# A scan-and-GeGLU kernel: the first weight rows second in the load queue, an activation tile on another queue, and tile 0's first products ahead of tile 1's transposes

## The chip, the core and the metric

The kernel runs on one NeuronCore of one Trainium2 chip. The metric is the device time of one execution in microseconds (us), the median of several executions; lower is better. Short names for the engines: PE is TensorE (matmul; PEld its weight loads), DVE VectorE, ACT ScalarE, POOL GpSimd, SP SyncE.

## The reference

```python
xn = _layernorm(x)                       # x: 1 x 2048 x 512, eps 1e-5, no affine part
s = _A_ref(xn, ...)                      # diagonal complex state space layer, 512 states
g = _silu((_gelu(xn @ w_gate) * (xn @ w_up)) @ w_down)      # F = 1376
return x + s * g
...
def _A_ref(x, ...):
    dt = exp(log_dt); Lam_bar = exp(dt * Lam); B_bar = ((Lam_bar - 1) / Lam)[:, None] * Bmat
    h_t = Lam_bar * h_{t-1} + B_bar x_t          # over 2048 steps
    y_t = 2 Re(C h_t) + Dskip * x_t
```

All inputs and the output are bfloat16.

## The kernel before

The 2048 tokens are four groups of 512, and each group is four tiles of 128 tokens. Per tile there are the products with w_up and w_gate (four row blocks of 128, columns cut at 512, 1024 and 1376), the GELU and the product of both on ACT and DVE, a transpose by DMA, and the product with w_down. Per group there are the products with B, a rotated real scan on DVE in place of the complex recurrence, and the products with C. PE is the engine that is hardly ever idle.

The program is written as a list of steps; each step belongs to an engine and emits its instructions. `Plan.run` emits them in the order of the tuple `ORDER`, which is written out in full. Each engine executes its own steps strictly in that order, so a step that waits holds up everything behind it on its engine. Nothing in `ORDER` is decided at run time; the times given to `load_x`, `load_w`, `dma` and the like are remarks of the plan and change no instruction.

This document is about the first microseconds, group 0, whose tiles are prepared by hand instead of by DMA:

- SP issues the loads one after the other: `load_x` (line 222) loads one tile of x (128 x 512, 128 KB), `load_w` (line 213) a block of a weight. The first 1024 columns of w_up come as four row blocks of 256 KB, called blocks 0 to 3 here; the other columns, the last tile of x, w_gate and B follow. ACT issues three loads of 1 KB each (line 256: log_dt, Lambda_im, Lambda_re).
- `dummies` (line 299) and `fill` (line 303) are products of constants which PE runs while nothing has landed. Their results are not used.
- `center(m)` takes the mean of tile m (tile 0: lines 339 and 341, shared by ACT and DVE; tiles 1 and 2: line 347 on ACT) and subtracts it on DVE (lines 343 and 348) into `xna`.
- `head_t(m)` transposes the centred tile on PE into PSUM and copies it into `xcT` (shown as the tile W, whose memory it uses): tile 0 in two halves, PE line 313, copies on DVE (line 319) and ACT (line 321); tiles 1 and 2 whole, PE line 328, copy on DVE (line 330).
- `parameters()` transposes the three small loads on PE (lines 603 and 604) and casts them on DVE (line 606); POOL and DVE go on from there to the decay and the angles.
- `up_rows(m, k)` (line 388) multiplies tile m by block k of w_up: two products of 512 columns, accumulated over k in two PSUM banks. `squares(m)` (line 352, ACT) and `stats(m)` (lines 280 and 281, DVE) give the variances; POOL makes the scale (lines 289 to 292), and ACT applies it when it evicts the finished sums (`out_up`, line 398).
- `first_w` (line 418) are the remaining products of group 0 with w_up and w_gate.

PE's order at the head is: `dummies`, `fill`, the transposes of tile 0, the transposes of tile 1, `parameters`, `up_rows(0, 0)`, the transposes of tile 2, `up_rows(1, 0)`, `(1, 1)`, `(0, 1)`, `(2, 0)`, `(2, 1)`, `(0, 2)`, `(1, 2)`, `(0, 3)`, `(1, 3)`, `(2, 2)`, `(2, 3)`, then `first_w`. DVE's is: centring of tile 0, centring of tile 1, copy of tile 0's first half, centring of tile 2, copy of tile 1, parameter cast, copy of tile 2. ACT's is: mean part of tile 0, mean of tile 1, mean of tile 2, copy of tile 0's second half, squares of tiles 1 and 2.

The loads report to eight semaphores in turn; a later load is issued on one of them only when the earlier load on the same one has landed.

Of the kernel before, what the change touches and what calls it, by code (L numbers as in the profile page):

```python
# [17 lines left out]
PE, ACT, DVE, POOL, SP = "PE", "ACT", "DVE", "POOL", "SP"  # L18


ORDER = (
# [23 lines left out]
)  # L45


# [33 lines left out]
def kernel(  # L81
# [17 lines left out]
    nc = tc.nc  # L99
    P = 128  # L100
    S = 2048
    D = 512
    F = 1376
    KT = D // P
# [3 lines left out]
    TS = 512  # L108
# [12 lines left out]
    V, A, G, T = nc.vector, nc.scalar, nc.gpsimd, nc.tensor  # L121
# [9 lines left out]
    x_tok = sb("x_tok", [P, NS * M, D])  # L131
    xnT = sb("xnT", [P, 2, M, KT, P])
    wg = sb("wg", [P, KT, F])
    wu = sb("wu", [P, KT, F])
# [3 lines left out]
    pv0, pv1 = sb("pv0", [4, P]), sb("pv1", [8, P])  # L138
# [52 lines left out]
    def dma(eng, issue, land, emit, reads=(), writes=(), **kw):  # L191
        return pl.add(eng, issue, emit, reads, writes, lag=land, **kw)

    TURN, SLAB = (3, 2.28, 1.5), (2, 1.5, 1.0)
    x_r = A_x[0].rearrange("(m p) d -> p m d", p=P)
# [14 lines left out]
    def load_w(nm, k0, k1, c0, c1, end, landed):  # L210

        w, r = w_of[nm]
        dma_sp(end, landed, lambda: nc.sync.dma_start(out=w[:, k0:k1, c0:c1], in_=r[:, k0:k1, c0:c1]),
               [(nm, k, c) for k in range(k0, k1) for c in range(3) if c0 <= CH[c][0] < c1])
# [6 lines left out]
    def load_x(m, end, landed):  # L221
        dma_sp(end, landed, lambda: nc.sync.dma_start(out=x_tok[:, m, :], in_=x_r[:, m, :]), [("x", 0, m)])  # L222

    W2 = CH[1][1]
    load_x(0, 1.12, 2.92)
    load_x(1, 1.59, 3.35)
    load_x(2, 2.06, 3.75)
    load_w("wu", 0, 1, 0, W2, 2.53, 5.1)
    load_w("wu", 1, 2, 0, W2, 3.0, 6.3)
    load_w("wu", 2, 3, 0, W2, 3.5, 7.4)  # L230
    load_w("wu", 3, 4, 0, W2, 4.0, 7.9)
    load_w("wu", 0, KT, W2, F, 4.5, 9.2)
    load_x(3, 5.0, 9.6)
    load_w("wg", 0, KT, 0, TS, 5.5, 11.0)
    load_w("wg", 0, KT, TS, F, 6.0, 13.5)
    for ri, src in enumerate((A_B_re, A_B_im)):
        dma(SP, 2.0, 3.0, lambda ri=ri, src=src: nc.sync.dma_start_transpose(out=BT[:, ri, :, :], in_=src), writes=[("BT", ri)],
            after=list(sp_last), svc=TURN)
# [13 lines left out]
    one = nc.const_aps.tensor(1.0, [P, 1], FP32)  # L252

    first = [acts(1, lambda: act(out=tiny[:], in_=one, func=AF.Silu), [], ["tiny"], rank=910.0, not_before=0.72)]
    for i, (t, v) in enumerate(((pv0[0:4, :], A_log_dt), (pv1[0:4, :], A_Lambda_im), (pv1[4:8, :], A_Lambda_re))):
        first = [dma(ACT, 0.48, 1.7, lambda t=t, v=v: A.dma_start(out=t, in_=v.rearrange("(k p) -> k p", p=P)),
                     writes=[("pv", i)], rank=900.0, not_before=0.8, after=first)]
    iota_i = sb("iota_i", [P, NBA], I32)
    iota_f = small("iota_f", NBA)

# [41 lines left out]
    def fill(w, i):  # L302
        pe(1, w, lambda: T.matmul(ring[i][:, 0:w], lhsT=warm[:, 0:P], rhs=warm[:, 0:w], start=True, stop=True), [], [("bank", i)])
# [347 lines left out]
    fill(256, 3)  # L651
    center(0)
    head_t(0)
    parameters()
    for m in range(1, M - 1):
        center(m)
# [187 lines left out]
```

## Time and profile before

| | us |
|---|---|
| median of 3 runs (lowest to highest) | 178.61 (178.25 to 178.89) |
| the profiled execution, its own time | 178.7 |
| its span in the trace | 176.9 |
| PE busy | 172.5 |
| DVE busy | 157.0 |
| ACT busy | 123.6 |
| POOL busy | 11.3 |

The span runs from the first to the last instruction of the program in the trace; the execution's own time contains 1.8 us more. All times inside the execution are counted from the start of the span. Matmuls are pipelined, so the duration shown for one contains its latency, and the distance from start to start says more. The mean granted clock of the profiled execution was 0.998.

### The profile page before, as it was taken

To read this page: it belongs to the slowest core of one execution; us is meant where nothing else is said; L and a number is where in the kernel's file an instruction comes from. 1 tells how busy PE (TensorE), PEld (TensorE's weight loads), DVE (VectorE), ACT (ScalarE), POOL (GpSimd) and SP (SyncE) were. 2 spreads that over 40 slices of the span, in tenths; PEclk is the share of its full clock that TensorE was granted. 3 is DMA by queue.
4 is the path that set the end of the run, shared out by engine and by line. 5 is a ranking of instruction groups with operands and counts; after the bars stand their busy time and mean duration, and the time that the engine had idled before them with its cause. 6 is when DMAs were issued, how large, how long until landed. Compare 5 with 4: busy or idle time off the path is not lost.

```text
span 176.9 us, 2419 instructions
## 1 busy us (share of the span) xinstructions
PE 172.5 (98%) x846; PEld 82.5 (47%) x846; DVE 157.0 (89%) x252; ACT 123.6 (70%) x236; POOL 11.3 (6%) x25
## 2 busy tenths in 40 slices
PE   8999999999999999999999999999999999999992
PEld 3454554444455544444445454444444455444451
DVE  2869999999698993999979999899999999999764
ACT  5589979979999999799578855373158618572240
POOL 2580030000200000000040000000000000000000
PEclk9999999999999999999999999999999999999999
DMA  5999999997000809423000075094000006617112
GB/s 145 318 369 241 207 239 261 181 266 163 0 0 0 200 1 186 98 78 63 0 0 6 30 126 105 30 192 85 0 0 0 0 30 156 70 38 157 41 60 77
DMA packets 48355, 18.66 MB, mean 105 GB/s; under 512 B 40312, under 2 KB 47832, under 8 KB 48344
## 3 DMA queue, kind: packets, MB, share of 16 engines
q1 hardware_dynamic: 48320, 18.52, 47.3%
q8 instruction: 6, 0.10, 0.2%
q14 instruction: 5, 0.04, 0.1%
q10 hardware_dynamic: 24, 0.00, 0.0%
HBM read 6.46 MB, written 2.10 MB: 48 GB/s over the span
## 4 chain that ended last, share of the span: by engine, by line
PE 94%; DVE 2%; DMA 1%; ACT 0%; issue 0%; SPq 0%; DVEq 0%
PE ring L449 32%; PE ring L481 22%; PE ring L547 16%; PE ybank L497 15%; PE ring L418 5%; PE ring L388 3%; PE ybank L418 2%; DMA x_tok<-in_A_x_dram 1%; DVE yg L502 1%; DVE junk L508 1%; PE ybank L328 0%; ACT junk L347 0%; SPq L222 0%; DVE xna L348 0%; PE ring L603 0%
## 5 line engine op out<-in xcount | busy, mean ns | idle before, releaser
L449 PEld LDWEIGHTS <-xnT 128*128 128x128 bf16 x288 | 28.2, 98 | 28.4
L481 PE MATMUL ring<-wd,atT 128*128 128x512 bf16 (+1 forms) x176 | 39.3, 379 | 0.0
L449 PE MATMUL ring<-wg,xnT 128*128 128x512 bf16 (+1 forms) x144 | 31.6, 357 | 0.0
L449 PE MATMUL ring<-wu,xnT 128*128 128x512 bf16 (+1 forms) x144 | 31.3, 357 | 0.0
L547 PE MATMUL ring<-xnT,BT 128*128 128x512 bf16 x128 | 30.1, 379 | 0.0
L578 DVE TENSOR_TENSOR_SCAN Fs<-rho,ini,W 128x512 bf16<-128x512 f32 x24 | 29.6, 1269 | 0.1
L452 ACT ACTIVATE ub<-ring 128x512 bf16<-128x512 f32 (+1 forms) x36 | 19.2, 555 | 14.2 <-PE ring L449 14.0
L497 PE MATMUL ybank<-C,hst 128*128 128x512 bf16 x120 | 27.7, 379 | 0.0
L481 PEld LDWEIGHTS <-atT 128*128 128x128 bf16 (+1 forms) x176 | 17.2, 98 | 20.8
L549 ACT ACTIVATE U<-ring 128x512 bf16<-128x512 f32 x32 | 18.3, 600 | 7.5 <-PE ring L547 7.5
L452 ACT ACTIVATE gt<-ring 128x512 bf16<-128x512 f32 (+1 forms) x36 | 19.5, 556 | 3.7 <-PE ring L449 3.5
L497 PEld LDWEIGHTS <-hst 128*128 128x128 bf16 x136 | 13.3, 98 | 14.0
L547 PEld LDWEIGHTS <-BT 128*128 128x128 bf16 x128 | 12.5, 98 | 14.7
L484 ACT ACTIVATE g<-ring 128x512 f32<-128x512 f32 x16 | 9.4, 595 | 14.3 <-PE ring L481 14.2
L559 DVE TENSOR_TENSOR Q<-U,tab 128x4096 bf16<-128x4096 bf16 x8 | 18.3, 2290 | 0.9 <-ACT tab L646 0.7
L559 DVE TENSOR_TENSOR Q<-Fs,tab 128x4096 bf16<-128x4096 bf16 x8 | 18.3, 2286 | 0.1
L502 DVE TENSOR_TENSOR yg<-ybank,g 128x512 bf16<-128x512 f32 x15 | 10.2, 685 | 5.8 <-PE ybank L497 5.7
L762 ACT ACTIVATE junk<-x_tok 128x512 bf16<-128x512 bf16 x16 | 10.0, 632 | 0.7 <-DMA x_tok<-in_A_x_dram 0.7
L493 ACT ACTIVATE ybank<-sk 128x512 f32<-128x512 bf16 x15 | 9.1, 605 | 1.7 <-DVE yg L502 1.6
L767 ACT ACTIVATE xna<-x_tok,nb,rs 128x512 bf16<-128x512 bf16 x12 | 9.5, 812 | 0.0
L578 DVE TENSOR_TENSOR_SCAN Fs<-rho,W 128x512 bf16<-128x512 f32 x8 | 9.3, 1210 | 0.1
L458 DVE TENSOR_TENSOR at<-gt,ub 128x1024 bf16<-128x1024 bf16 x12 | 8.2, 683 | 0.1
(140 smaller groups left out, 170.1 us busy)
## 6 DMA issues: line engine op xcount, KB each, us to landing
x_tok<-in_A_x_dram SPq DMA_DIRECT2D x3, 512.0 KB, 4.3
out_dram<-ot SPq DMA_DIRECT2D x12, 128.0 KB, 1.8
wd<-in_B_w_down_dram SPq DMA_DIRECT2D x1, 1280.0 KB, 7.1
wu<-in_B_w_up_dram SPq DMA_DIRECT2D x4, 256.0 KB, 4.2
wg<-in_B_w_gate_dram SPq DMA_DIRECT2D x1, 864.0 KB
x_tok<-in_A_x_dram SPq DMA_DIRECT2D x4, 128.0 KB, 2.5
wg<-in_B_w_gate_dram SPq DMA_DIRECT2D x1, 512.0 KB, 5.4
wu<-in_B_w_up_dram SPq DMA_DIRECT2D x1, 352.0 KB, 4.9
```

The source lines that it names most:

```text
L418: T.matmul(ps[:, 0 : b - a], lhsT=lhs(k), rhs=wt[:, k, a:b], start=(k == 0), stop=(k == KT - 1))
L449: T.matmul(ps[:, 0 : b - a], lhsT=xnT[:, s % 2, m, k, :], rhs=wt[:, k, a:b], start=(k == 0), stop=(k == KT - 1))
L452: acts(b - a, lambda: act(out=dst[:, a:b], in_=ps[:, 0 : b - a], func=AF.Copy if up else AF.Gelu_apprx_tanh), [("bank", r)], [key], table= ...
L481: T.matmul(ps[:], lhsT=atT[:fs, k, m * P : (m + 1) * P], rhs=wd[:fs, k, :], start=(k == 0), stop=(k == NFT - 1))
L497: T.matmul(ps, lhsT=hst[s % 2][:, j // NPT, j % NPT, m * P : (m + 1) * P], rhs=C2[:, j // NPT, j % NPT, c0:c1], start=(j == 0 and not seed ...
L502: dve(w, lambda: V.tensor_tensor(out=yg[e][:, c0:c1], in0=ps, in1=g2[gi][:, b, c0:c1], op=ALU.mult), [key, ("g2", gi, b)], [("yg", e, c0)])
L547: T.matmul(ps[:], lhsT=BT[:, ri, k, pt * P : (pt + 1) * P], rhs=xnT[:, s % 2, :, k, :], start=(k == 0), stop=(k == KT - 1))
L549: acts(512, lambda q=q, ri=ri, ps=ps: act(out=U[ui][:, ri, q, :], in_=ps[:], func=AF.Copy), [("bank", r)], [("U", ui, q, ri)])
L559: dve(4096, lambda: V.tensor_tensor(out=Qf, in0=src.unsqueeze(1).to_broadcast(WQ), in1=table, op=ALU.mult), reads, ["Q"], rate=2.0)
L578: pl.add(DVE, 1.12 if s == 0 else 1.185, lambda ri=ri, q=q, pt=pt, first=first: V.tensor_tensor_scan(out=Fs[:, ri, q, :], data0=rho[:, pt ...
L762: acts(512, lambda i=i, fn=fn, sc=sc, m=m: act(out=junk()[:], in_=x_tok[:, s * M + m, :], func=fn, scale=sc, accum_out=sx[:, s, i, m : m + ...
L767: acts(512, lambda m=m: act(out=xn[m], in_=x_tok[:, s * M + m, :], func=AF.Identity, scale=rs[:, s, m : m + 1], bias=nb[:, s, m : m + 1]), ...
```

## The change

On SP's queue the load of x's tile 1 is gone; block 0 of w_up comes second, x's tile 2 third, then one of the small loads (Lambda_re), then blocks 1, 2 and 3 and the rest as before. On ACT's queue x's tile 1 is loaded after the first small load (log_dt) and ahead of Lambda_im.

PE's order at the head becomes: `dummies`, `fill`, the transposes of tile 0, a second `fill` of 256 columns, `up_rows(0, 0)`, the transposes of tile 1, `parameters`, `up_rows(0, 1)`, `(1, 0)`, the transposes of tile 2, `(1, 1)`, `(0, 2)`, `(2, 0)`, `(2, 1)`, `(1, 2)`, `(0, 3)`, `(1, 3)`, `(2, 2)`, `(2, 3)`, then `first_w`. DVE's becomes: centring of tile 0, copy of tile 0's first half, centring of tile 1, copy of tile 1, parameter cast, centring of tile 2, copy of tile 2. ACT's becomes: mean part of tile 0, mean of tile 1, copy of tile 0's second half, mean of tile 2, squares of tiles 1 and 2.

All steps behind these stand in `ORDER` as before; their numbers are one higher, because the second filler is one step more. The diff, with `ORDER` cut to its head:

```diff
 ORDER = (
-    21, 22, 23, 24, 25, 0, 28, 26, 20, 18, 19, 17, 1, 41, 15, 16, 13, 14, 2, 43, 3, 4, 5, 29, 30, 42, 6, 7, 27, 31, 32, 61, 35, 34, 45, 46, 33, 63,
-    44, 65, 62, 64, 69, 68, 36, 66, 67, 70, 71, 72, 74, 77, 73, 80, 83, 85, 47, 48, 37, 38, 39, 49, 50, 51, 53, 52, 56, 55, 75, 87, 76, 78, 79, 54,
...
+    20, 21, 22, 23, 25, 0, 28, 42, 26, 19, 17, 18, 16, 1, 14, 15, 12, 13, 2, 24, 3, 4, 29, 30, 5, 6, 27, 31, 32, 35, 34, 44, 46, 47, 33, 64, 43, 62,
+    36, 69, 63, 65, 37, 45, 66, 70, 72, 67, 68, 71, 73, 75, 78, 74, 81, 84, 86, 48, 49, 38, 39, 40, 50, 51, 52, 54, 53, 57, 56, 76, 88, 77, 79, 80,
...
 )
...
     load_x(0, 1.12, 2.92)
-    load_x(1, 1.59, 3.35)
-    load_x(2, 2.06, 3.75)
-    load_w("wu", 0, 1, 0, W2, 2.53, 5.1)
-    load_w("wu", 1, 2, 0, W2, 3.0, 6.3)
-    load_w("wu", 2, 3, 0, W2, 3.5, 7.4)
-    load_w("wu", 3, 4, 0, W2, 4.0, 7.9)
-    load_w("wu", 0, KT, W2, F, 4.5, 9.2)
-    load_x(3, 5.0, 9.6)
-    load_w("wg", 0, KT, 0, TS, 5.5, 11.0)
-    load_w("wg", 0, KT, TS, F, 6.0, 13.5)
+    load_w("wu", 0, 1, 0, W2, 1.59, 4.2)
+    load_x(2, 2.06, 4.4)
+    load_w("wu", 1, 2, 0, W2, 2.9, 5.5)
+    load_w("wu", 2, 3, 0, W2, 3.3, 6.4)
+    load_w("wu", 3, 4, 0, W2, 4.6, 7.2)
+    load_w("wu", 0, KT, W2, F, 5.0, 9.0)
+    load_x(3, 5.4, 9.4)
+    load_w("wg", 0, KT, 0, TS, 5.9, 10.8)
+    load_w("wg", 0, KT, TS, F, 6.4, 13.3)
...
-    for i, (t, v) in enumerate(((pv0[0:4, :], A_log_dt), (pv1[0:4, :], A_Lambda_im), (pv1[4:8, :], A_Lambda_re))):
-        first = [dma(ACT, 0.48, 1.7, lambda t=t, v=v: A.dma_start(out=t, in_=v.rearrange("(k p) -> k p", p=P)),
-                     writes=[("pv", i)], rank=900.0, not_before=0.8, after=first)]
+    rows = lambda v: v.rearrange("(k p) -> k p", p=P)
+    dma(ACT, 0.48, 1.7, lambda: A.dma_start(out=pv0[0:4, :], in_=rows(A_log_dt)), writes=[("pv", 0)], rank=900.0, not_before=0.8)
+    dma(ACT, 0.43, 2.2, lambda: A.dma_start(out=x_tok[:, 1, :], in_=x_r[:, 1, :]), writes=[("x", 0, 1)])
+    dma(ACT, 0.48, 1.7, lambda: A.dma_start(out=pv1[0:4, :], in_=rows(A_Lambda_im)), writes=[("pv", 1)], rank=900.0)
+    dma(SP, 0.48, 1.7, lambda: nc.sync.dma_start(out=pv1[4:8, :], in_=rows(A_Lambda_re)), writes=[("pv", 2)], rank=900.0)
...
     center(0)
     head_t(0)
+    fill(256, 3)
     parameters()
```

42 rows, old and new, of the table ORDER are left out of this document.

## The prediction

> **What bounds the kernel now.** I read the page first, then the chain of waits, then the timeline of the first seven microseconds, engine by engine.
>
> ```profile
> span 176.9 us, 2419 instructions
> ...
> PE 172.5 (98%) x846; PEld 82.5 (47%) x846; DVE 157.0 (89%) x252; ACT 123.6 (70%) x236; POOL 11.3 (6%) x25
> ...
> PE 94%; DVE 2%; DMA 1%; ACT 0%; issue 0%; SPq 0%; DVEq 0%
> ```
>
> PE is busy in 172.5 of 176.9 us and carries 94% of the chain. Only two PE waits are listed: 0.8 us before the first warm-up product, and 0.4 us before tile 1's transposes. So the end is set by the moment from which products run without a gap, plus the work then left. The chain of waits, from 2 to 7 us, shows what sets that moment:
>
> ```profile
> 1.18 2.59 DMA x_tok<-in_A_x_dram
> ...
> 3.79 0.36 ACT junk L347
> ...
> 4.55 0.36 DVE xna L348
> ...
> 4.96 0.61 PE ybank L328 x4
> ...
> 5.70 0.54 PE ring L388 x2
> 6.24 0.22 PE ybank L328 x4
> 6.46 0.65 PE ring L388 x3
> ```
>
> It starts with x's second tile landing at 3.77, passes its mean (ACT), its centring (DVE) and tile 1's transposes, and only then reaches tile 0's first products. The timeline gives the starts:
>
> ```profile
> 3.92 0.62 PE L313 MATMUL ring<-ident,xna 128*128 128x128 bf16 x4
> ...
> 4.55 0.35 DVE L348 TENSOR_SCALAR xna<-x_tok,ma 128x512 bf16<-128x512 bf16 x1 [0.68 <-ACT junk L347]
> ...
> 4.82 0.28 DVE L319 COPY W<-ring 128x256 bf16<-128x256 bf16 x1
> ...
> 4.96 0.61 PE L328 MATMUL ybank<-ident,xna 128*128 128x128 bf16 x4 [0.41 <-DVE xna L348]
> ...
> 5.50 0.18 PE L603 MATMUL ring<-ident,pv 4*128 4x4 bf16 x1
> ...
> 5.64 0.60 PE L388 MATMUL ring<-wu,W 128*128 128x512 bf16 x2
> ...
> 6.08 0.39 PE L328 MATMUL ybank<-ident,xna 128*128 128x128 bf16 x4
> ...
> 6.30 4.91 PE L388 MATMUL ring<-wu,W 128*128 128x512 bf16 x22
> ...
> 11.05 1.36 PE L418 MATMUL ybank<-wu,W 128*128 128x352 bf16 x8
> ```
>
> The 22 products from 6.30 start 0.216 us apart ((11.05 − 6.30) / 22) and PE waits for nothing afterwards. So the figure to compare is the first start of L418: 11.05. I write up(m,k) for the two products of tile m with row block k of w_up.
>
> **The landings.** Issue plus time to landing, for one DMA at a time: x tile 0 at 0.72 + 2.0 = 2.75; tile 1 at 3.77; tile 2 at 4.12; row blocks 0 to 3 at 5.49, 6.65, 7.38 and 8.06; the rest of w_up at 9.1. Now up(0,0) starts 0.15 after block 0 landed, and up(1,1), the first use of block 1, at 6.30 + 2 × 0.216 = 6.73, 0.08 after that landed: two covers that are nearly used up.
>
> **The change, step by step.** (1) The DVE copy of tile 0's first transposed half goes ahead of tile 1's centring. The first two transposes end at 4.33 (3.92 + 0.41 for two), so the copy runs 4.40 to 4.68 instead of 4.82 to 5.10. ACT's copy of the second half goes ahead of tile 2's mean; it is needed only by blocks 2 and 3.
>
> (2) The second filler is 256 columns; the fillers of 512 start 0.43 us apart (2.34 us for five, the last's latency included), so it costs about 0.21 at 4.34 to 4.55, while PE waits for step 1. Nothing, unless the copy came earlier than 4.55.
>
> (3) Block 0 is issued second. Its bound from below is 4.12, the landing of the third 128 KB piece when 384 KB had been asked for; from above its present 5.49, behind 640 KB. With x0 ahead of it and x1 beside it on the other queue 512 KB are asked for, half-way between 384 and 640: 4.80. Up(0,0) then starts at 4.88, not 5.64: 0.76 earlier.
>
> (4) This is where the gain goes. At 4.88 products still start 0.43 apart: tile 1's transposes (4.96 to 5.25, three steps of 0.097) are slow, tile 2's at 6.08 and up(0,0) at 5.64 are at the full pace. Taking the change of pace at about 5.5, up(0,0) holds PE to 5.65. Tile 1's transposes, queued behind it, start at 5.65 instead of 4.96. Their data is there if x1 lands by 4.46 (its way from landing to L328 took 4.96 − 3.77 = 1.19). On ScalarE's queue it is the second issue, at about 1.38 where the second small load is issued now; by time to landing 2.0 to 2.6 at 3.4 to 4.0, up to 4.8 if it shares the engines with block 0 to the end. I take 4.3.
>
> (5) Transposes 5.65 to 5.87, last result 6.03 (0.22 latency at the full pace), DVE copy 0.42: tile 1 is ready for up(1,0) at 6.07 + 0.42 + 0.06 = 6.55, against 6.30 now. In between come the parameter transposes (0.38 from the last transpose to the next product now, 5.25 to 5.64; I take 0.3) and up(0,1), 6.12 to 6.55. That is no gap.
>
> (6) From 6.55 there are left 20 products and tile 2's transposes: 20 × 0.216 + 0.22 = 4.54, so L418 starts at 11.09. Before: 11.05. Sum: +0.04 us. The first row is 0.76 us earlier, but tile 1's turn is 0.69 later and the continuous run begins at the same time: the products put ahead ran at half pace in time in which tile 1 would have been prepared.
>
> (7) Block 1 is now wanted at 6.12, not 6.73. Its bytes ahead (x0, x1, x2, block 0: 640 KB) are the same. Bounds: 6.65 as now; and, if the second queue lifts the stretches
>
> ```profile
> 1.70:2.50 0.80, 0.80 (x4) 0.24 (x3) 0.00 (x0) 0.50 (x2) 0.19 (x1) 1.00 0.79 200
> 2.50:3.50 1.00, 1.00 (x4) 0.36 (x3) 0.61 (x3) 0.40 (x2) 0.00 (x0) 1.00 1.00 260
> 3.50:4.50 1.00, 1.00 (x6) 0.36 (x4) 0.36 (x1) 0.71 (x3) 0.00 (x0) 1.00 0.85 226
> 4.50:5.50 1.00, 0.58 (x5) 0.35 (x5) 0.89 (x3) 1.00 (x5) 0.00 (x0) 1.00 0.98 320
> ```
>
> (last column GB/s) to the 320 of the last line, 917 KB have moved by 2.5 + 757/320 = 4.9, and with tile 2's lag of 0.7 it lands at 5.6. I take 6.0, the middle, which just does not decide. Each 0.1 beyond 6.04 costs 0.1, because PE's queue is in order and up(1,0), ready at 6.55, stands behind up(0,1). Block 2 is wanted at 7.63 and landed at 7.38. The Trainium skill, "DMA: Bandwidth & Descriptors", section "Issuing engines are not separate DMA queues", says that a second issuing engine saves only issue time, as all transfers run on the same 16 DMA engines. The DMA share of 1.00 and 0.98 in two of these rows agrees, the 0.79 and 0.85 in the others leave some room; by that rule alone the sum would be +0.65.
>
> (8) Other moves. One small parameter load goes to SyncE between x2 and block 1: its issue takes 0.26 to 0.31, a weight issue 0.43, and block 1 stays fifth there, so its issue is no later than 2.59. Block 3's issue, which now waited for x1 (3.77, issued 3.79), would wait for the second load of its queue, block 0 (4.80): with 4.3 to landing 9.1, wanted at about 9.3 (up(0,3) is at 9.32 now). Behind it on SyncE are the rest of w_up, x's last tile and w_gate: the rest lands at 9.1 plus up to 0.7, wanted at 11.05; w_gate's first part at 10.9 plus as much, wanted at 12.84. Covered, by a second or more; uncovered they would cost what they are late.
>
> (9) DVE and POOL: the parameter cast moves from 5.95 to about 6.5, tile 0's statistics from 6.84 to about 7.8, the angles with them; ACT's first eviction goes from 9.80 to about 10.2, the DVE tables by up to 0.9. PE wants that bank back at 12.24 (evicted at 10.5 now), the transposed inputs at 19.81 and 24.46 (issues at 11.94 and 13.28, SyncE's turn ends before 21), and DVE has 1.65 us idle between 44.2 and 48.6. So I charge nothing; without that cover it would be up to 0.9.
>
> **The rivals.** *Row block 1 comes late (slower).* It stays at 6.65 because the same bytes are ahead; up(0,1) starts at 6.73, up(1,0) at 7.16, and L418 at 7.16 + 4.54 = 11.70: +0.65, 179.2. For it: the DMA share near 1. Against: the slow stretches at 200 and 226 GB/s. It exceeds 0.3% from a landing of about 6.55.
>
> *The pace changes earlier (faster).* If products run at 0.216 from 4.7 on and x1 lands by 3.9, with block 0 by 4.6 and block 1 by 5.5, then up(0,0) is 4.74 to 5.17, the transposes end at 5.39 and their last result at 5.56, up(0,1) is 5.64 to 6.07, up(1,0) at 5.56 + 0.52 = 6.08: L418 at 10.62, −0.43, 178.2. Before hardly gains from this: its chain is set by x1 and block 1. For it: the filler removes part of a 0.41 us gap. Against: products were still slow at 5.25. The Trainium skill, "TensorE: Matmul & The Clock Gate", section "Part 1: The HAM clock gate (the "warmup" mystery)", has the clock doubling after about 3.4 us of activity, in a window that is not tied to the kernel's start; the trace's change between 5.25 and 5.64 fits, the page would let it fall elsewhere in another execution.
>
> *The change does not do what it says.* x1 is slow on ScalarE's queue, 4.8 instead of 4.3: its transposes then start at 4.8 + 1.19 = 5.99, 0.34 after step 4's 5.65, and all that follows with them: 178.9.
>
> **How the numbers follow.** The profiled execution took 178.7 us, 1.8 beside its span, against a median of 178.61. The forecast, +0.04 on that, is 178.6; its own range is 178.2 to 179.0, from step 7 and the pace. I give it 0.40, late block 1 0.30, the earlier pace 0.24 and the last 0.06. The range 177.9 to 179.3 takes in both sides, with some 0.2 for the runs' own spread (178.25 to 178.89). 0.3% is 0.54 us, about what a measurement of this kernel can tell from no change. Faster by more: half of the earlier pace, whose price of 0.43 falls short of it by less than the spread, 0.12. Slower by more: the late block, 0.30. The rest, 0.58, is within.
>
> **What would show it.** L418's first start near 11.05. Step 1: L319 at 4.4. Step 3: the first L388 near 4.9. Step 4: L328 first at about 5.6, no longer released by L348. Step 7: a PE gap before the second pair of L388 released by a wu DMA would mean the slower rival; L388 pairs 0.22 apart before 5.2 the faster one. A PE gap after 12 us would refute step 9.

## The result, and the profile after

| | before | after |
|---|---|---|
| median of 22 executions each, us | 178.68 (178.25 to 180.08) | 179.42 (179.04 to 181.21) |
| profiled execution: own time, span, us | 178.7, 176.9 | 179.4, 177.7 |
| first start of the first rest product (L418, after L419), us | 11.05 | 11.78 |

The change makes the kernel slower: ratio 1.0044 with a 95% interval of 1.0031 to 1.0058. The forecast was no change, 178.6, and 179.42 lies above its range (177.9 to 179.3). In the kernel after every line number from the change on is one higher (L388 is L389, L418 is L419).

The page after, in the places shown of before:

```profile
span 177.7 us, 2421 instructions
...
PE 173.5 (98%) x847; PEld 82.5 (46%) x847; DVE 156.8 (88%) x252; ACT 123.3 (69%) x236; POOL 11.4 (6%) x25
...
PE 94%; DMA 2%; DVE 2%; ACT 1%; issue 0%; DVEq 0%
```

The execution's own time grew by 0.7 and PE's busy time by 1.0, for one filler more: by the page PE is not idle longer, it is longer at nearly the same work. The shares of the chain have nearly not moved, so the place must be looked for. From the first start of L418 or L419 to the end of the span it is 165.9 us in both profiles (176.9 − 11.05; 177.7 − 11.78). The whole difference lies ahead of that start. The chain of waits of the kernel after, up to 8 us (start, duration, what):

```profile
1.37 3.55 DMA x_tok<-in_A_x_dram
...
4.94 0.36 ACT junk L348
...
5.70 0.36 DVE xna L349
...
6.11 0.61 PE ybank L329 x4
...
6.86 0.98 PE ring L389 x4
7.84 0.22 PE ybank L329 x4
```

It is the same chain as before, x's tile 1 through mean and centring to its transposes, and it starts from a load that lands at 4.92 instead of 3.77. It takes 1.19 us from there to the transposes (6.11 − 4.92), to the hundredth what it took before. The timeline of the same stretch (start, duration, engine, line; in brackets the idle time before it and what ended it):

```profile
4.07 0.61 PE L314 MATMUL ring<-ident,xna 128*128 128x128 bf16 x4
...
4.50 0.29 DVE L320 COPY W<-ring 128x256 bf16<-128x256 bf16 x1 [0.49 <-PE ring L314]
...
4.85 1.03 PE L389 MATMUL ring<-wu,W 128*128 128x512 bf16 x2
...
6.11 0.61 PE L329 MATMUL ybank<-ident,xna 128*128 128x128 bf16 x4 [0.22 <-DVE xna L349]
...
6.65 0.18 PE L604 MATMUL ring<-ident,pv 4*128 4x4 bf16 x1
...
6.79 1.05 PE L389 MATMUL ring<-wu,W 128*128 128x512 bf16 x4
...
7.68 0.39 PE L329 MATMUL ybank<-ident,xna 128*128 128x128 bf16 x4
...
7.90 4.05 PE L389 MATMUL ring<-wu,W 128*128 128x512 bf16 x18
...
11.78 0.46 PE L419 MATMUL ybank<-wu,W 128*128 128x352 bf16 x2
```

Compared with before, stretch by stretch, from tile 0's transposes (L313, L314) on: they start 0.15 later (x's tile 0 landed at 2.89 instead of 2.75). PE then waits or runs fillers 0.38 and 0.43 + 0.14 us, together 0.95, against 0.62 + 0.14 = 0.76 before: +0.19. Up(0,0) holds PE for 0.83 instead of 0.44, as products still start 0.43 apart: +0.39. The rest is equal to 0.01. The sum is 0.15 + 0.19 + 0.39 = 0.73, which is what L419 is later (11.78 − 11.05). Read along the chain, the same 0.73 is tile 1's landing, 1.15 later (4.92 − 3.77), less the 0.42 that is saved behind its transposes, where up(0,0) no longer stands (5.67 from there to L419 instead of 6.09). So the 0.39 is no cause by itself: at full pace PE would have waited longer for tile 1. The 0.22 in the bracket of L329 counts from PE's modelled end; by starts, PE was free from about 5.68 (5.25 + 0.43).

The landings show what the transfers gave and took: block 0 at 4.56 instead of 5.49, x's tile 1 at 4.92 instead of 3.77, tile 2 at 5.27 instead of 4.12, blocks 1 and 2 at 5.94 and 6.69 instead of 6.65 and 7.38, block 3 at 8.19 instead of 8.06.

### The profile page after: what moved, and what is told of

It is laid out like the page before. It is cut to its first block, busy times and chain, and to the rows that moved or that the text cites. A ratio compares the mean times of both kernels' runs of the same rounds, so it can differ in the third digit from the quotient of the medians.

```text
span 177.7 us, 2421 instructions
## 1 busy us (share of the span) xinstructions
PE 173.5 (98%) x847; PEld 82.5 (46%) x847; DVE 156.8 (88%) x252; ACT 123.3 (69%) x236; POOL 11.4 (6%) x25
## 4 chain that ended last, share of the span: by engine, by line
PE 94%; DMA 2%; DVE 2%; ACT 1%; issue 0%; DVEq 0%
PE ring L450 31%; PE ring L482 21%; PE ring L548 16%; PE ybank L498 15%; PE ring L419 5%; PE ring L389 3%; PE ybank L419 2%; DMA x_tok<-in_A_x_dram 2%; DVE yg L503 1%; DVE junk L509 1%; PE ybank L329 0%; ACT L253 0%; ACT junk L348 0%; DVE xna L349 0%; PE ring L604 0%
## 5 line engine op out<-in xcount | busy, mean ns | idle before, releaser
L503 DVE TENSOR_TENSOR yg<-ybank,g 128x512 bf16<-128x512 f32 x15 | 10.2, 686 | 5.8 <-PE ybank L498 5.7
```

Of the source, the lines that this page charges most:

```text
L503: dve(w, lambda: V.tensor_tensor(out=yg[e][:, c0:c1], in0=ps, in1=g2[gi][:, b, c0:c1], op=ALU.mult), [key, ("g2", gi, b)], [("yg", e, c0)])
```

## The experiments

My theory after the result: x's tile 1 now comes late, and products ahead of its turn run at half pace (starts of 512 columns 0.43 apart instead of 0.216). The rivals: the order of the steps is worse by itself; the late change of pace is the cause; block 1 comes late. The start of L418 or L419 in each profile ("the head") is compared with before's 11.05; times are medians beside the median of the kernel before on the same chip. The ratio comes with its 95% interval; it is not simply the quotient of the two medians (178.83 to 179.28 in the first run is 1.0025, its ratio 1.0043).

### Each half alone

The new order of the steps and the second filler, on the loads of before:

```diff
-    load_w("wu", 0, 1, 0, W2, 1.59, 4.2)        # and x's tile 1 on ACT's queue
+    load_x(1, 1.59, 3.35)                       # on SP's queue; block 0 behind tile 2
```

> The changed kernel with the old loads: x's tile 1 second and block 0 fourth on SyncE's queue, all small loads on ScalarE's; the new order of steps and the second filler stay. Theory A (the loss is tile 1's late preparation, and it is late because x's tile 1 lands late on ScalarE's queue): tile 1 is centred at 4.9 again, but its transposes stand behind tile 0's products, which wait for block 0 (5.5), so they start at 6.0 to 6.4, and L419 at 11.4 to 11.8: 0.35 to 0.7 us over before. Theory B (the order of steps alone costs the loss, whatever the loads): 0.7 to 0.8 over before, a gap in front of tile 0's first products. Theory C (the loads alone): within 0.2 of before.

Measured: 179.28 beside 178.83, ratio 1.0043 (1.0015 to 1.0072). PE's waits and its timeline in this run:

```profile
PE ring L389 <- DMA wu<-in_B_w_up_dram: 0.9, 1, 0.9
```

```profile
5.41 0.59 PE L389 MATMUL ring<-wu,W 128*128 128x512 bf16 x2 [0.92 <-DMA wu<-in_B_w_up_dram]
5.84 0.39 PE L329 MATMUL ybank<-ident,xna 128*128 128x128 bf16 x4
```

Here x's tile 1 landed at 3.25 and its transposes could have been done in the 0.92 us in which PE waited for block 0. The written order keeps them behind up(0,0). Head 11.30, although products ran at full pace from 3.58 on in this profile. The median is 0.45 above before, and the ratio is that of the whole change.

The new loads under the steps of before (no second filler; the lines are shown as an edit of the kernel before):

```diff
-    load_x(1, 1.59, 3.35)
+    load_w("wu", 0, 1, 0, W2, 1.59, 4.2)        # x's tile 1 on ACT's queue, as in the change
```

> The changed kernel with the old order of steps on PE, DVE and ACT and without the second filler; the new loads stay. Theory A: x's tile 1 lands at 4.9 as in the changed kernel, tile 1's transposes start at 6.1, and tile 0's products now stand behind them, idle time before: tile 1's products with block 0 near 7.3, L419 near 11.9 to 12.1, 0.9 to 1.1 us over before, more than the whole change. Theory B: back at before, within 0.2. Theory C: 0.7 to 0.8 over before, as the change.

Measured: 180.38 beside 178.83, ratio 1.0094 (1.006 to 1.0129). The profile has PE waiting 1.7 us for L349, the centring of tile 1, whose load landed at 5.11. Head 12.18.

```profile
PE ybank L329 <- DVE xna L349: 1.7, 1, 1.7
```

The ten executions fall in two groups, 179.15 to 179.87 and 180.90 to 181.43. So neither half wins, and the two halves are not a gain and a loss that cancel. The losses don't add either: 0.45 for the order alone and 1.55 for the loads alone, against 0.74 for both.

The change without its second filler:

```diff
-    fill(256, 3)       # the one behind head_t(0)
```

> The changed kernel without the second filler. Theory A: the filler lies in PE's wait for tile 0's copy; the time is that of the changed kernel within 0.1. Theory D (the filler delays the real work, or is what moved the change of PE's pace from 5.54 to 6.77): faster than the changed kernel by 0.2 or more, with the change of pace back before 6.

Measured: 179.99 beside 178.83, ratio 1.0081 (1.005 to 1.0112). Neither outcome that was expected came: it is slower than the change. Its profile looks better than the change's (head 11.43), and six of its twelve executions take 179.09 to 179.58. The other six take 180.39 to 181.27. One in 22 executions of the change is that long. The prediction had the filler as costing nothing. In the profile it does cost nothing (the copy ends after it), but without it half of the executions are long; no profile shows what the long executions do.

### The load of x's tile 1

The change, with x's tile 1 issued ahead of log_dt on ACT's queue (0.79 instead of 1.37):

```diff
 ORDER = (
-    20, 21, 22, 23, 25, ...
+    20, 22, 21, 23, 25, ...
```

> The changed kernel with one swap on ScalarE's queue: x's tile 1 ahead of the first small load, so it is issued at about 0.78, ahead of block 0's issue at 1.18 instead of behind it (1.37). If the DMA engines serve the loads of both queues in the order of their issue: x's tile 1 lands at 3.4 to 3.8, tile 1's transposes follow tile 0's products directly at 5.6 to 5.7, and L419 starts at 11.0 to 11.2: 0.5 to 0.7 us less than the changed kernel, within 0.2 of before, plus what tile 0 itself may land later (2.9 to 3.2) by sharing. If ScalarE's queue as such is slow (served behind SyncE's): it lands after 4.4 and at most 0.2 is won.

Measured: 179.10 beside 178.83, ratio 1.0014 (0.9998 to 1.003). Most of the loss is gone: 0.27 above before, where the change is 0.74 above it. Tile 1 landed at 3.46 and tile 0 at 3.20, which is 0.3 to 0.45 later than in the other profiles; both transfers now run at once. Block 0 landed at 4.12, and tile 1's transposes follow up(0,0) without a wait:

```profile
5.15 1.03 PE L389 MATMUL ring<-wu,W 128*128 128x512 bf16 x2
5.97 0.46 PE L329 MATMUL ybank<-ident,xna 128*128 128x128 bf16 x4
...
11.50 1.36 PE L419 MATMUL ybank<-wu,W 128*128 128x352 bf16 x8
```

Head 11.50 in a profile whose own time, 180.03, was the longest of its twelve executions; it has a later PE wait of 0.5 us for w_down.

Tile 1 centred from tile 0's data, so that nothing waits for its load (in this run and the others that take a wait away, the products concerned are not the reference's):

```diff
-        x = x_tok[:, m, :]
+        x = x_tok[:, 0 if m == 1 else m, :]
```

> The changed kernel with tile 1 centred from tile 0's data (its mean and its centring read x's tile 0; all loads, instructions and orders stay), so nothing at the head waits for x's tile 1; the rows of tile 1 are then not the reference's. Theory A (the landing of x's tile 1 on ScalarE's queue is the loss): tile 1's transposes start as soon as tile 0's products let them, 5.6 to 5.7 instead of 6.11, L419 at 11.1 to 11.3, 0.4 to 0.6 us less than the changed kernel, 0.2 to 0.4 over before. Theory D (the pace of PE is the loss): at most 0.2 less than the changed kernel. If tile 0's products standing ahead is the whole loss: no gain at all.

Measured: 179.30 beside 178.67, ratio 1.0042 (1.0022 to 1.0061): no gain, against what my theory asked for. The timeline shows why:

```profile
5.76 0.63 PE L329 MATMUL ybank<-ident,xna 128*128 128x128 bf16 x4
...
6.81 1.02 PE L389 MATMUL ring<-wu,W 128*128 128x512 bf16 x4 [0.28 <-DMA wu<-in_B_w_up_dram]
...
11.78 1.36 PE L419 MATMUL ybank<-wu,W 128*128 128x352 bf16 x8
```

The transposes start 0.35 earlier than in the change, and then up(0,1) waits for block 1, which landed at 6.77 in this execution: the head is 11.78 again. (In the run before, where the swap of the loads did gain, block 1 landed at 6.09.) Two waits end nearly together. So the other was taken away alone, and then both:

```diff
-    T.matmul(t[:], lhsT=..., rhs=wu[:, k, a:b], ...)
+    T.matmul(t[:], lhsT=..., rhs=wu[:, 0 if k == 1 else k, a:b], ...)
```

> The changed kernel with the second pair of products of each tile fed with block 0 instead of block 1 (block 1 is still loaded; these products are not the reference's); the wait for x's tile 1 stays. Theory F: tile 1's transposes stay at 6.1 to 6.3 and L419 at 11.7 to 11.8, within 0.2 of the changed kernel. If block 1 alone is the bound: 0.25 to 0.5 less than the changed kernel.

Measured: 179.62 beside 178.58, ratio 1.006 (1.0031 to 1.009); head 11.50, the transposes of tile 1 at 6.04 behind L349. Nothing gained.

> The changed kernel with tile 1 centred from tile 0's data and the second pair of products of each tile fed with block 0 instead of block 1, so that the head waits neither for x's tile 1 nor for block 1 (both are still loaded; the products concerned are not the reference's). Theory F (two waits of about the same end, x's tile 1 at 4.9 to 5.1 and block 1 at 6.0 to 6.8, so that taking one away alone leaves the other): tile 1's transposes at 5.7, the second pair of products right after the parameters at 6.3 to 6.5, L419 at 11.2 to 11.5, 0.25 to 0.5 us less than the changed kernel. Theory G (neither counts; the half pace of tile 0's products ahead is the whole loss): the time of the changed kernel within 0.15.

Measured: 179.04 beside 178.58, ratio 1.0022 (1.0008 to 1.0035). Head 11.05, which is the prediction's 11.09 to 0.04:

```profile
4.79 0.96 PE L389 MATMUL ring<-wu,W 128*128 128x512 bf16 x2
5.59 0.39 PE L329 MATMUL ybank<-ident,xna 128*128 128x128 bf16 x4
...
6.04 1.06 PE L389 MATMUL ring<-wu,W 128*128 128x512 bf16 x4
...
11.05 1.36 PE L419 MATMUL ybank<-wu,W 128*128 128x352 bf16 x8
```

The profiled execution took 178.71, near the lowest of its twelve (178.64). Beside the kernel before as it is, about half of the loss goes by the ratios (1.0044 to 1.0022), and 0.28 of 0.74 by the medians. That is the two waits' share of the loss only if the kernel before would gain nothing from the same edits, which the next run asks.

### Is it the order?

To see the order without any of these waits, they were taken away in the kernel before too, and in the new order on the old loads; the edits are the two just shown.

> The control: the kernel before with the same two waits taken away (tile 1 centred from tile 0's data, second pair of products fed with block 0). Its tile 0 products still wait for block 0 at 5.3 to 5.5, so little can be won: L418 at 10.8 to 11.1, 0 to 0.2 us less than before. More than 0.3 less would mean that before, too, is bound by x's tile 1 or block 1, and that taking them away from the changed kernel hid part of its loss.

Measured: 178.69 beside 179.01, ratio 0.9969 (0.9933 to 1.0005). Head 10.35. By the medians the kernel before gains 0.32 without these waits, with an interval that includes no gain. The 0.70 at the head is not the waits' doing: in this execution tile 1 landed at 3.30 and block 1 at 5.71, so that waiting for tile 1 would have cost about 0.1 (an estimate: 3.30 + 1.19 = 4.49 against 4.40) and for block 1 nothing, while block 0 landed at 4.90 instead of 5.49. With both waits gone in both kernels the medians of the change and of before differ by 0.35 as they stand, and by 0.78 each beside its own before (0.46 above, 0.32 below). How much of the loss the two waits make in the median is therefore not settled: it lies between about half and nothing.

> The new order of steps and the second filler on the old loads, tile 1 centred from tile 0's data and the second pair of products fed with block 0 (the products concerned are not the reference's). If the order by itself costs time: tile 0's products wait for block 0 (4.9 to 5.4), tile 1's transposes and the parameters, ready at 4.4, stand behind them and are done after 5.4 instead of before; L419 0.4 to 0.7 later than in the kernel before with the same waits gone, 0.2 to 0.5% over it, at or above the kernel before. If only the loads count: equal to the kernel before with the same waits gone, about 0.3% under before.

Measured: 178.97 beside 178.75, ratio 1.0023 (1.0002 to 1.0044). Head 11.03. The two timelines, first the order of before, then the new one:

```profile
4.40 0.41 PE L328 MATMUL ybank<-ident,xna 128*128 128x128 bf16 x4
...
4.95 0.59 PE L388 MATMUL ring<-wu,W 128*128 128x512 bf16 x2
...
10.35 1.36 PE L418 MATMUL ybank<-wu,W 128*128 128x352 bf16 x8
```

```profile
5.15 0.59 PE L389 MATMUL ring<-wu,W 128*128 128x512 bf16 x2 [0.27 <-DMA wu<-in_B_w_up_dram]
5.58 0.39 PE L329 MATMUL ybank<-ident,xna 128*128 128x128 bf16 x4
...
11.03 1.36 PE L419 MATMUL ybank<-wu,W 128*128 128x352 bf16 x8
```

The old order does tile 1's transposes and the parameters' while block 0 is on its way, the new one after it has been used: 0.68 at the head of these two profiles. Of that, 0.20 is the later start of up(0,0) (5.15 against 4.95), as block 0 landed at 5.11 in the one and at 4.90 in the other; 0.48 comes behind that start. The medians, each beside its own kernel before, differ by 0.54 (0.22 above and 0.32 below) and by 0.28 as they stand (178.97 − 178.69, on two chips). The two intervals just overlap, and seven of the 23 executions of before beside the first were above 180.4 and raise its median. That the order costs by itself is seen in the profiles and suggested by the times, not settled by them.

The new loads in the old order, with both waits gone, and then with tile 2 also taken from tile 0's data:

```diff
-        x = x_tok[:, 0 if m == 1 else m, :]
+        x = x_tok[:, 0, :]
```

> The new loads with the old order of steps and no second filler, tile 1 centred from tile 0's data and the second pair of products fed with block 0 (the products concerned are not the reference's). If the rest of the loss is the new order of steps (tile 0's products at half pace ahead of tile 1's transposes): tile 1's transposes at 4.4 to 4.7, tile 0's products at 4.8 to 5.2, L419 at 10.7 to 11.0, 0.3 to 0.6 us less than the changed kernel with both waits away, at or below before. If it lies in the loads or behind the head: within 0.15 of the changed kernel with both waits away.

Measured: 179.07 beside 179.01, ratio 1.0022 (0.9988 to 1.0055). Head 11.56: tile 2's transposes wait to 6.47, since its load landed at 5.2. A third tile of the new loads comes late.

> The old order of steps, no second filler, on the new loads, with tiles 1 and 2 centred from tile 0's data and the second pair of products fed with block 0 (the products concerned are not the reference's), so that PE waits at the head for x's tile 0 and block 0 alone. If x's tile 2, now behind block 0 and x's tile 1, was what held h1: tile 2's transposes directly behind tile 0's products at 5.5 to 5.8, L419 at 10.3 to 10.9, 0.3 to 0.6 us less than h1 and 0.2 to 0.4% under before. If the loads cost time otherwise (tile 0 landing later, work behind the head): within 0.15 of h1.

Measured: 178.95 beside 178.75, ratio 1.0009 (0.9996 to 1.0022). Head 10.84, and then a wait that is hidden elsewhere, the first line of PE's waits:

```profile
PE ring L482 <- DMA wd<-in_B_w_down_dram: 1.2, 1, 1.2
```

w_down landed at 32.46, and its first product, with nothing else to wait for, would have started 1.2 earlier. It landed at 29.34 in the profile before, with its first use at 31.36, and at 30.84 after, with its first use at 32.10: the change takes 0.8 of the 2.0 us that covered it. Does that cost anything in the median? Two runs moved w_down's large load one place forward on SP's queue, one on the last kernel and one on the change (shown for the change):

```diff
-    ..., 176, 185, 154, 115, 231, ...
+    ..., 176, 185, 115, 154, 231, ...
```

> The old order of steps on the new loads with tiles 1 and 2 centred from tile 0's data and the second pair of products fed with block 0, as before, and the large load of w_down one place earlier on SyncE's queue, ahead of the first transpose of the gated product (1.4 us of issue time). If late w_down is part of what holds this kernel: w_down lands at 29.5 to 31.0, no PE wait at 31 to 33, 178.3 to 178.7, 0.2 to 0.5 us less than with w_down in its old place. If w_down is late in few executions only: the median within 0.15 of it.

> The changed kernel with the large load of w_down one place earlier on SyncE's queue, nothing else. The head is untouched, so L419 stays at 11.3 to 11.8. If the head is the whole loss, as in the profiled execution of the changed kernel (w_down 1.3 us ahead of its first use): within 0.15 of the changed kernel, 0.35 to 0.5% over before. If late w_down is part of it: 0.2 us or more less.

Measured: 179.00 beside 178.59, ratio 1.0023 (1.0006 to 1.0041), and 179.40 beside 178.59, ratio 1.0041 (1.0027 to 1.0055). Neither is better than the kernel it was made from, though in the first w_down landed at 29.67 again and the wait was gone (head 11.30). A late w_down holds up single profiled executions (1.2 us here, 0.5 with tile 1's load first); in these medians no part of the loss is seen to come from it.

### The pace of the products

Three instead of seven warm-up products in the kernel before:

```diff
-    dummies(7, 3)
+    dummies(3, 3)
```

> The kernel before with three instead of seven products of constants at the start, so PE idles from about 2.2 to 3.6. Theory D: PE's pace changes later in more executions, some or most of them at 7.5 to 9.5, and these are 0.8 to 1.7 us above the kernel before, in a second group of times; the profile shows half pace well beyond 6.5. If the pace does not depend on the early products: within 0.15 of before, one group.

Measured: 180.88 beside 178.67, ratio 1.0132 (1.0098 to 1.0166). The timeline shows the half pace last:

```profile
4.08 0.61 PE L313 MATMUL ring<-ident,xna 128*128 128x128 bf16 x4 [1.67 <-DVE xna L343]
...
7.04 6.00 PE L388 MATMUL ring<-wu,W 128*128 128x512 bf16 x22
```

The same 22 products that took 4.91 take 6.00. Within the group the starts are 0.43 apart up to 9.23 and 0.216 apart from there. Idle PE in the first 4 us is paid later. (The trace's clock records give the moment: full pace from 9.23 here, from 5.54 in the profile before and 6.77 in that of the change.)

Two fillers in the change between up(0,0) and tile 1's transposes:

```diff
+            if m == 1:
+                for _ in range(2):
+                    T.matmul(ring[3][:, 0:256], lhsT=warm[:, 0:P], rhs=warm[:, 0:256], start=True, stop=True)
```

> The changed kernel with two more products of constants (256 columns each) between tile 0's products and tile 1's transposes, where PE waits for x's tile 1 (5.68 to 6.11 in its trace). Theory D (idle time at the head lets the change of PE's pace slip by a whole window, which costs up to 1.7 us in some executions): no execution 1 us or more above the others, and the median as the changed kernel's or up to 0.3 less. Theory A alone: the same as the changed kernel within 0.15.

Measured: 179.43 beside 178.67, ratio 1.0038 (1.0013 to 1.0064): the change's own time. In this profile the pace changes at 5.57 and not at 6.77, and the transposes start at 6.32, because x's tile 1 landed at 5.13. In the change's profile the half pace of up(0,0) lies in the wait for the late load and costs nothing more; the half pace of the transposes and parameters behind it costs 0.21. The two fillers gain nothing in the median. Whether the pace has a part in the change's median is not shown, as no run sets the pace by itself.

### Versions that might have won

The change with tile 1's load back in second place on SP's queue and block 0 third, tile 1's transposes ahead of up(0,0) again and the parameters' behind it; the same with block 1 ahead of tile 2; and the kernel before with the parameter transposes put into the wait for tile 1:

```diff
-    load_w("wu", 0, 1, 0, W2, 1.59, 4.2)
-    load_x(2, 2.06, 4.4)
+    load_x(1, 1.59, 3.35)
+    load_w("wu", 0, 1, 0, W2, 2.06, 4.6)        # then tile 2, or block 1 and tile 2
```

```diff
-    ... 4, 5, 29, 30, 42, 6, 7, 27, 31, 32, 61, 35, 34, 45, 46, 33, 63, ...
+    ... 4, 5, 29, 30, 6, 7, 27, 31, 32, 33, 42, 35, 61, 34, 45, 46, 63, ...
```

> A candidate: x's tile 1 second on SyncE's queue, block 0 third, x's tile 2 fourth, all small loads on ScalarE's queue; DVE's and ACT's copies of tile 0 early and the second filler as in the change; on PE tile 1's transposes again ahead of tile 0's products, then the parameters, tile 1's products with block 0, tile 2's transposes and the rest. Theory A: x's tile 1 lands at 3.3 to 3.8, block 0 at 4.6 to 5.0, tile 1's transposes start at 4.6 to 5.0, tile 1's first products at 5.8 to 6.1, L419 at 10.7 to 11.0: 0.1 to 0.4 us less than before. If block 1 lands after 6.5 or the pace changes late, as before within 0.2.

> A candidate: SyncE's queue in the order x's tile 0, tile 1, block 0, block 1, x's tile 2, block 2 and so on, small loads on ScalarE's queue; on PE the first transposes, the second filler, tile 1's transposes, tile 0's products with block 0, the parameters, tile 1's with block 0, both tiles' with block 1, tile 2's transposes, both tiles' with block 2, then tile 2's. If the DMA engines serve in order of issue: block 0 lands at 4.5 to 4.9, block 1 at 5.5 to 6.0, x's tile 2 at 5.9 to 6.4; tile 1's transposes start at 4.6 to 5.0 and PE runs on without a wait from there; L419 at 10.8 to 11.1, 0 to 0.25 us less than before. A block 1 after 6.6 or an x tile 2 after 6.6 would put it at or above before.

> The kernel before with one move: the parameters' transposes stand on PE ahead of tile 1's, in the gap from 4.54 to 4.96 where the small loads have landed, and the DVE copy of tile 0's first half ahead of tile 1's centring. Nothing else changes. Tile 0's first products then wait for block 0 alone (5.3 to 5.5): they start at 5.4 to 5.6 instead of 5.64, and L418 at 10.9 to 11.05 where block 1 is there by 6.5: 0 to 0.15 us less than before. If the waits at the head are set by block 1 anyway: the same as before within 0.1.

Measured: 179.06 beside 178.67, ratio 1.0022 (1.0006 to 1.0038), head 11.40, with block 1 landing at 7.05; 178.71 beside 178.58, ratio 1.0016 (0.9997 to 1.0034), head 10.79; 178.64 beside 178.58, ratio 1.0005 (0.9991 to 1.0019), head 11.12. None beats the kernel before, although gains of up to 0.4, 0.25 and 0.15 were expected. The second had a head 0.26 ahead of before in its profile, and still no gain in the median: its profiled execution, 178.44, was among its quick ones.

## Why the prediction was wrong, step by step

**Right:** step 1, the copy L320, was 4.40 in the prediction and 4.50 in the profile, with x's tile 0 0.14 later. Step 3: block 0 landed at 4.56 (4.80 said), up(0,0) began at 4.85 (4.88) and held PE to 5.68 (5.65). That start is luck in part: it was set by the copy L320 (4.50 to 4.79), and not by block 0, which had been there for 0.29. Step 6: from up(0,1) to L419 it was 5.00 (4.97). Steps 8 and 9: no PE wait after 12 us, with ACT's first eviction at 10.78 (10.2 said) and the DVE tables at 15.72, 1.3 later instead of up to 0.9.

**Right by luck, step 7.** Block 1 landed at 5.94 (6.0 said, 6.04 wanted). In the ten other profiles with the same loads it came at 6.14 to 7.40, so it would have been late for the prediction's plan in every one of them. The working slipped as well: the middle of the bounds 5.6 and 6.65 is 6.1, not 6.0.

**Wrong, step 4, the landing of x's tile 1.** Taken at 4.3 with bounds of 3.4 and 4.8, it was 4.92; with the 1.19 of its way the transposes came at 6.11 and not at 5.65: 0.46. They were again released by the centring (L349), the sign that the prediction had named against this step. The error was to take the time from issue to landing that x's tiles had on the other queue (2.0 to 2.6; it took 3.55), with an equal share of the engines as the worst case. In all 20 profiles x's first three tiles and the parts of w_up landed in the order of issue, whichever engine issued them: block 0 at 4.56, 4.92, 4.43, 4.91, 4.19 and tile 1 at 4.92, 5.11, 4.64, 5.10, 4.43 (the change, the new loads alone, no filler, no wait for tile 1, no wait for both). It was issued 0.2 behind block 0 and landed behind its 256 KB each time. The packets in the trace of the change say the same: those of block 0 start from 2.26 to 4.11, those of tile 1 from 3.49 to 4.49, the first of them 2.1 after the issue. Issued ahead of block 0 it landed ahead of it (3.46 and 4.12), and most of the loss was gone. The rule that the prediction cited in step 7 for block 1, the Trainium skill, "DMA: Bandwidth & Descriptors", section "Issuing engines are not separate DMA queues", says that transfers of all issuing engines run on the same 16 DMA engines and interleave there. The landings agree with the first half, which should have been applied to step 4. Interleaving would let a small load overtake a large one; the packets of the two ran side by side only from 3.49 to 4.11, and in no profile here did one of these loads land ahead of one issued before it.

**Wrong, the pace in steps 4 and 5.** Taken to change at 5.5, it changed at 6.77. Tile 1's transposes and the parameters held PE 0.68 and not the 0.47 said (6.12 − 5.65): 0.21. With the 0.46 that is 0.67 of the 0.69 between 11.09 and 11.78. This term moves from execution to execution: with two fillers in the wait the pace changed at 5.57, and the head was 11.78 all the same, with tile 1 landing 0.21 later.

**The rivals.** The third, a slow x1 on ScalarE's queue, had the right mechanism with a price of 0.34 and a chance of 0.06. The first, a late block 1, had a chance of 0.30: absent in the profile of the change, it decided as soon as tile 1 was not waited for. Where both are late, the later one sets the time; the two do not add. With both gone the head was 11.05, as steps 5 and 6 had it, in a profile whose pace changed at 5.55, where the prediction had put it. So for the head the sum was sound and its inputs were not; the median of that run, 0.46 above before, is not explained by it. The range ended at 179.3, because each rival was priced alone: a late tile (0.46) together with a late pace (0.21) was not among them.

**Step 8 asked the wrong thing of the transfers.** It went through the queue for what is wanted late, and found cover. But what one load gains, others lose: 0.93 us gained for block 0, 1.15 lost for each of x's tiles 1 and 2. The bytes moved from 1.7 to 5.5 us were about the same, 0.97 MB by the prediction's four rows and 1.05 MB by the same four rows after:

```profile
1.70:2.50 0.80, 0.80 (x4) 0.25 (x3) 0.00 (x0) 0.50 (x2) 0.19 (x1) 1.00 0.95 190
2.50:3.50 1.00, 1.00 (x4) 0.38 (x3) 0.56 (x2) 0.40 (x2) 0.00 (x0) 1.00 0.78 125
3.50:4.50 1.00, 1.00 (x7) 0.43 (x5) 0.41 (x1) 0.00 (x0) 0.00 (x0) 1.00 1.05 375
4.50:5.50 1.00, 1.00 (x5) 0.15 (x3) 0.29 (x1) 0.56 (x2) 0.00 (x0) 1.00 1.06 400
```

The rate is not fixed within the stretch: from 2.5 to 3.5 it was 125 GB/s instead of 260, and why is open. Before, the tile's turn ran in the wait for block 0; after, block 0's products stand in the wait for the tile.

**One profile as the base.** The prediction took the chain of before from x's tile 1 landing at 3.77. In the seven other profiles that load it second on SP's queue it landed at 3.25 to 3.44. So it is not shown that the wait of 0.41 us for tile 1, on which the prediction builds, is typical of the kernel before.

**Open:** what the second group of long executions is (in e2 and e5 half of them; its times are those of f2, whose half pace lasts to 9.23, but no profile of e2 or e5 fell into it), and how the loss in the median divides between the order and the loads. The head is accounted for to the hundredth, but in one execution of each kernel.

## What to carry to other kernels

In all profiles of this kernel a load that was put on another engine's queue still landed behind what was issued before it; when one is moved forward, list whom it passes and what those loads feed. Put work that needs early data into the wait for late data, and not behind the product that ends the wait. When two waits end within a few tenths of one another, an experiment that removes one may show nothing: remove both, and do the same in the kernel before, which may gain from it too.

## What the hardware showed that was not expected

- Two queues did not overtake one another: x's tile 1 (128 KB, ACT's queue, issued at 1.37) landed 0.36 after block 0 (256 KB, SP's queue, issued at 1.18) and 3.55 after its issue. Issued at 0.79, it landed at 3.46, and tile 0 landed at 3.20 instead of 2.75 to 2.91.
- The moment at which products double their pace was anywhere from 3.6 to 6.8 us with seven warm-up products, and 9.2 with three, by the clock records of these traces. The Trainium skill, "TensorE: Matmul & The Clock Gate", section "Part 1: The HAM clock gate (the "warmup" mystery)", ties the clock to recent activity; the three-product run agrees, with 2.2 us more in the median.
- With both waits removed the head of the change's profile came 0.73 us earlier (11.78 to 11.05), and its median 0.28 closer to before's (0.74 to 0.46). One profile is one execution: its head and its own time have to be read together.
